# Attention and two dense blocks: row maxima of the third and fourth query tile, one instruction per head

## Chip, cores and metric

The kernel runs on one core of one Trainium2 chip. The metric is the device time of one execution in microseconds (us). A core has five engines that work side by side, each through its own queue and in the order of that queue: TensorE (PE, matrix products), VectorE (DVE), ScalarE (ACT), GpSimd (POOL) and SyncE (SP, which here only issues transfers). They wait for each other with semaphores.

## What is computed

The reference is causal attention with a memory term, and two dense blocks behind it. The part that the change touches is the softmax of the attention:

```python
B, H, S, D = q.shape                       # 4, 8, 576, 64
scores = scale * np.matmul(q, k.transpose(0, 1, 3, 2))
scores = np.where(causal, -1000000000.0, scores)
scores = scores - scores.max(-1, keepdims=True)
a = np.exp(scores)
a /= a.sum(-1, keepdims=True) + 1e-09
local = np.matmul(a, v)
...
x = _moe_ref(x=x, **moe_kwargs)            # ((x @ w1) * (x @ w2)) @ w3 @ w_out
return _moe2_ref(x=x, **moe2_kwargs)       # h = x @ w_in; (h - tanh(h)) @ w_out
```

The attention's result is mixed with the memory term by a gate of each head before the dense blocks.

## The kernel before

The work runs in three stages. In the first, the attention, the 32 pairs of batch and head are taken two heads at a time: 16 pairs P, each with 576 queries cut into five query tiles. A unit n is one pair and one query tile u, so there are 80 units. For u from 0 to 3 a tile holds 128 queries and sees K = 128 (u + 1) keys; u = 4 holds the last 64 queries of both heads, one head on each half of the partitions. The second stage is the first dense block (with the rest of the memory term), the third is the second dense block.

For a unit the steps are these, with the names that the loop over `ORDER` uses:
- S: `scores` (PE) writes both heads' scores into a PSUM tile `sc` of [128, 2, 512], one bank for each head, and adds the causal mask by a product with the identity. There are two such tiles, so the scores of unit n + 2 need the tile of unit n. Then `rmax` (line 343, DVE) takes the negated maximum of each row into the tile `st`; one instruction reads both heads and writes two columns.
- E: `exps` (line 352, ACT) has one instruction for each head: the exponential of the scores with the maximum as bias, written to `p`, and the row sum into a further column of `st` (for u = 4 one instruction for both heads). In the trace each is followed by a short read of the accumulator.
- N: `norm` adds 1e-9 to the sums and takes the reciprocal (lines 361 and 362, DVE), and POOL scales `p` (line 369).
- T: `trans` (lines 401 to 412), one unit later: PE transposes `p`, and ACT or DVE copies the result out of PSUM (lines 380, 382).
- A: `av`, two units later: the products with v.
- L loads the q/k tile of a later pair and scales the next pair's q (line 196, ACT).
- G: background work from a generator, some two steps for each unit: the decoder of the 64-bit weights, whose steps alternate between ACT (line 74), DVE (lines 75, 77, 81, 84) and POOL (lines 96, 99), the product of two weight matrices (tiles `fo`, `s`, `wf`, lines 257 to 263), and the memory term of the first group of tokens (tiles `mw`, `mst`, lines 491 to 529).

The generator's instructions carry an edge that puts them behind the unit's own marked instruction on DVE and on ACT (`mark["V"]`, `mark["A"]`, used by `issue_after`). Beyond such edges, the order in each engine's queue is not that of the program: the context is opened with `schedule_with_timeline_sim=True`, which orders the instructions by a modelled timeline when the program is built. A change in the instructions can so change the order of others.

The lines that the change touches and those that read what it writes:

```python
mark["V"][n] = DV.tensor_reduce(out=st[:, 0:2] if u < 4 else st[:, 0:1], in_=seen(n),
                                axis=AX.X if u < 4 else AX.XY, op=ALU.max, negate=True).ins
...
for x in [slice(0, 1), slice(1, 2)] if u < 4 else [slice(0, 2)]:
    mark["A"][n] = AC.activation(out=p[:, x], in_=sc[:, x], func=AF.Exp, bias=st[:, x.start:x.start + 1],
                                 accum_out=st[:, 2 + x.start:3 + x.start]).ins
```

Of the kernel before, what the change touches and what calls it, by code (L numbers as in the profile page):

```python
# [18 lines left out]
ALU = mybir.AluOpType  # L19
AX = mybir.AxisListType  # L20
# [12 lines left out]
def block_kernel(ctx, tc, qk, qt, vt, mp, zp_d, beta, w1, w2, w3t, wo, wi, wo2, ident_d, mask_d, out):  # L33
    nc = tc.nc
    PE, DV, AC, PO, SP = nc.tensor, nc.vector, nc.scalar, nc.gpsimd, nc.sync
# [143 lines left out]
    V = [ap1.tile([128, 5, 2, 64], F32, name=f"v{i}") for i in range(2)]  # L179
# [87 lines left out]
    if True:  # L267
# [48 lines left out]
        mark = {"V": {}, "A": {}}  # L316
# [19 lines left out]
        def seen(n):  # L336
            P, u = units[n]
            return sc_t[n][:, :, 0:128 * (u + 1) if u < 4 else 288]

        def rmax(n):  # L340
            P, u = units[n]
            st = st_t[n] = ap4.tile([128, 8], F32, tag="st", name="st")
            mark["V"][n] = DV.tensor_reduce(out=st[:, 0:2] if u < 4 else st[:, 0:1], in_=seen(n),  # L343
                                            axis=AX.X if u < 4 else AX.XY, op=ALU.max, negate=True).ins

        def exps(n):
            P, u = units[n]
# [229 lines left out]
        def do(x, n):  # L577
# [3 lines left out]
            if x == "S":  # L581
                scores(n)
                rmax(n)
            elif x == "E":
                exps(n)
            elif x == "N":
                norm(n)
            elif x == "T":
                trans(n)
            elif x == "A" and u in (1, 4):  # L590
                av(P, u // 4)
                if u == 4 and P + 2 < 16:
                    load_v(P + 2)
            elif x == "L":
                if u == 0 and 1 <= P <= 16 - RB:
                    load_qk(P + RB - 1)
                if u == 2 and P < 15:
                    scale_q(P + 1)
            elif x == "G":
                bgc[0] += BG if n < MB else BG2  # L600
                with ExitStack() as s:
                    for e, k in TH:
                        if n - k >= 0:
                            s.enter_context(tc.issue_after(mark[e][n - k]))
                    while bgc[0] >= 1:
                        if next(bg, None) != 1:
                            bgc[0] -= 1
# [363 lines left out]
```

## Time and profile before

| what | value |
|---|---|
| median of 3 runs | 1025.48 us (1024.51 to 1026.22) |
| the profiled execution's own time | 1025.37 us |
| its span, first to last instruction | 1023.6 us |
| busy share of the span | PE 95%, DVE 74%, ACT 58%, POOL 36% |
| reductions of line 343 | 80 instructions, 63.8 us of DVE in all |
| exponentials of line 352 | 144 instructions, 78.3 us of ACT in all |
| ACT idle ahead of exponentials, ended by line 343 | 30.5 us, 32 times |
| granted TensorE clock | 0.995 of full speed over the span |

The profile is of one execution. Busy times are unions of an engine's instructions, so two that overlap count once. A wait is put down to the instruction that ended last before it. The chain of waits is followed back from the last instruction of the program: at each step to what released it, or to the instruction before it on its engine. `st<-sc` means that tile `st` is written from tile `sc`; shapes are partitions x elements. The attention stage takes about the first 256 us.

### The profile page before, as it was taken

Reading aid. Unit: us, or ns where it says so; the run is one execution under the profiler, and the core shown is the slowest. Engines: PE = TensorE matmul, PEld = TensorE weight load, DVE = VectorE, ACT = ScalarE, POOL = GpSimd, SP = SyncE. Lnnn points to the kernel's source line nnn. Section 1 sums busy time; section 2 is a strip of 40 time slices with the busy share of each in tenths; the row PEclk is TensorE's granted clock in tenths of the full one; section 3 lists DMA queues with packets and bytes.
Section 4 is the critical chain, followed back from the end, with each engine's and each line's share of the span. In section 5 each row is a group of like instructions: output and inputs, shape, how many; then the busy total and the mean of one; then the engine's idle time right before and its main releaser. Section 6 shows DMA issues by size and latency. Waiting matters only on the chain.

```text
span 1023.6 us, 15593 instructions
## 1 busy us (share of the span) xinstructions
PE 976.3 (95%) x5512; PEld 823.4 (80%) x5512; DVE 758.0 (74%) x1361; ACT 593.1 (58%) x1356; POOL 364.4 (36%) x396
## 2 busy tenths in 40 slices
PE   5999999989987989999999999999999999999998
PEld 2565565544876778999999989999999999989996
DVE  5868888787689996575212798878787787788875
ACT  5767766677323434233222458777676677767765
POOL 3646756486465212200000773222222222221221
PEclk9999999999999999999999999999999999999999
DMA  6434543343144652133000100000000000000000
GB/s 227 133 109 144 167 150 101 114 133 93 45 152 128 186 180 63 52 124 103 1 1 1 42 21 1 1 1 31 1 32 1 1 32 1 32 1 1 32 1 31
DMA packets 44237, 68.27 MB, mean 67 GB/s; under 512 B 4864, under 2 KB 30208, under 8 KB 44160
## 3 DMA queue, kind: packets, MB, share of 16 engines
q1 hardware_dynamic: 44160, 67.29, 20.8%
q8 instruction: 43, 0.70, 0.3%
q14 instruction: 34, 0.28, 0.1%
HBM read 62.56 MB, written 4.72 MB: 66 GB/s over the span
## 4 chain that ended last, share of the span: by engine, by line
PE 69%; DVE 18%; ACT 4%; issue 4%; DMA 3%; POOL 1%; SPq 0%; DVEq 0%; ACTq 0%; POOLq 0%
PE o L143 22%; PE h L143 20%; PE ab L143 13%; PE x L143 6%; DVE T L81 3%; PE sc L143 3%; PE fo L143 3%; DVE st L343 2%; DVE T L75 2%; ACT p L352 2%; DVE T L77 2%; PE t L401 2%; DMA r<-in_qk 1%; DVE T L84 1%; DMA mw<-in_qt 1%
## 5 line engine op out<-in xcount | busy, mean ns | idle before, releaser
L858 POOL TENSOR_TENSOR gl<-s,gh 128x384 fp32r<-128x384 f32 x96 | 99.8, 1039 | 295.3 <-ACT gh L852 286.3
L143 PE MATMUL ab<-xh,wa 128*128 128x384 f32 x384 | 108.6, 343 | 8.2 <-DVE xs L529 4.1
L369 POOL TENSOR_SCALAR p<-p,st 128x128 f32<-128x128 f32 (+2 forms) x144 | 94.2, 666 | 54.7 <-DVE st L362 21.7
L143 PE MATMUL x<-abh,wf 128*128 128x384 f32 x384 | 106.9, 342 | 2.7 <-ACT abh L656 2.1
L143 PE MATMUL ab<-xh,wb 128*128 128x384 f32 x384 | 106.2, 337 | 0.5 <-POOL wb L96 0.5
L352 ACT ACTIVATE p<-sc,st 128x128 f32<-128x128 f32 (+2 forms) x144 | 78.3, 549 | 45.1 <-DVE st L343 30.5
L834 DVE SCALAR_TENSOR_TENSOR s<-s,u 128x384 f32<-128x384 f32 x96 | 84.1, 876 | 22.8 <-ACT s L824 21.7
L143 PE MATMUL sc<-r 64*64 64x288 f32 (+4 forms) x384 | 76.1, 479 | 16.8 <-ACT p L352 11.0
L830 ACT ACTIVATE u<-u,pc 128x384 f32<-128x384 f32 x96 | 59.4, 619 | 46.5 <-DVE s L834 46.5
L74 ACT ACTIVATE T<-raw 128x512 f32<-128x512 f32 x72 | 48.2, 674 | 64.0 <-DMA raw<-in_wo 9.4
L653 DVE TENSOR_TENSOR a<-ab,a 128x384 f32<-128x384 f32 x48 | 26.5, 551 | 76.6 <-PE ab L143 76.6
L143 PEld LDWEIGHTS ab<-xh,wa 128*128 128x128 f32 x384 | 70.9, 190 | 12.4 <-DVE xs L529 5.3
L343 DVE TENSOR_REDUCE st<-sc 128x2 f32<-128x256 f32 (+4 forms) x80 | 63.8, 799 | 18.5 <-PE sc L143 17.3
L840 DVE TENSOR_TENSOR t<-h,t 128x384 f32<-128x384 f32 x96 | 53.3, 555 | 32.1 <-ACT t L823 31.7
L822 ACT ACTIVATE u<-h 128x384 f32<-128x384 f32 x96 | 47.0, 490 | 48.5 <-PE h L143 48.5
L143 PEld LDWEIGHTS x<-abh,wf 128*128 128x128 f32 x384 | 70.3, 189 | 4.5 <-ACT abh L656 3.2
L143 PEld LDWEIGHTS ab<-xh,wb 128*128 128x128 f32 x384 | 70.7, 189 | 1.2 <-POOL wb L96 1.2
L143 PE MATMUL x<-abl,wf 128*128 128x384 f32 x192 | 66.2, 345 | 3.9 <-DVE abl L657 3.9
L839 DVE SCALAR_TENSOR_TENSOR s<-s,s 128x384 f32<-128x384 f32 x96 | 62.9, 655 | 8.7 <-DVE s L834 0.5
L143 PE MATMUL ab<-xl,wa 128*128 128x384 f32 x192 | 65.5, 342 | 1.5 <-DVE xl L633 1.5
L846 DVE COPY_PREDICATED s<-u,t 128x384 f32<-128x384 uint32 x96 | 58.4, 609 | 9.0 <-ACT t L823 0.5
L143 PE MATMUL ab<-xl,wb 128*128 128x384 f32 x192 | 64.5, 336 | 0.0
(214 smaller groups left out, 2587.7 us busy)
## 6 DMA issues: line engine op xcount, KB each, us to landing
raw<-in_wo SPq DMA_DIRECT2D x24, 512.0 KB, 3.5
r<-in_qk SPq DMA_DIRECT2D x15, 576.0 KB, 3.9
raw<-in_w3t SPq DMA_DIRECT2D x16, 512.0 KB, 3.7
raw<-in_w SPq DMA_DIRECT2D x16, 512.0 KB, 3.8
raw<-in_wi SPq DMA_DIRECT2D x16, 512.0 KB, 3.7
v<-in_vt SPq DMA_DIRECT2D x16, 320.0 KB, 3.9
mw<-in_qt SPq DMA_DIRECT2D x18, 256.0 KB, 3.2
out<-ob SPq DMA_DIRECT2D x18, 256.0 KB, 2.3
```

Of the source, the lines that this page charges most:

```text
L74: AC.activation(out=tf, in_=hw.bitcast(F32), func=AF.Abs)
L143: return PE.matmul(o, lhsT, rhs, start=start, stop=stop).ins
L343: mark["V"][n] = DV.tensor_reduce(out=st[:, 0:2] if u < 4 else st[:, 0:1], in_=seen(n), axis=AX.X if u < 4 else AX.XY, op=ALU.max, negate= ...
L352: mark["A"][n] = AC.activation(out=p[:, x], in_=sc[:, x], func=AF.Exp, bias=st[:, x.start:x.start + 1], accum_out=st[:, 2 + x.start:3 + x. ...
L369: (DV if NV[u] == "V" else PO).tensor_scalar(out=pr, in0=pr, scalar1=sc, scalar2=1.0, op0=ALU.mult, op1=ALU.mult)
L822: AC.activation(out=u, in_=o, func=AF.Square)
L830: AC.activation(out=u, in_=u, func=AF.Relu, bias=pc[:, 2:3])
L834: DV.scalar_tensor_tensor(out=s1, in0=s1, scalar=k2[0], in1=u, op0=ALU.add, op1=ALU.mult)
L839: DV.scalar_tensor_tensor(out=s1, in0=s2, scalar=k2[1], in1=s1, op0=ALU.add, op1=ALU.mult)
L840: DV.tensor_tensor(out=t, in0=o, in1=t, op=ALU.subtract)
L846: DV.copy_predicated(out=s1, mask=u[:].bitcast(U32), data=t)
L858: PO.tensor_tensor(out=l, in0=s1, in1=h[:].bitcast(F32), op=ALU.subtract)
```

## The change

For u = 2 and u = 3 the maxima are taken by two instructions, the first over head 0's scores into the first column of `st`, the second over head 1's into the second column. The unit's mark on DVE is then the second of them. The other units keep one instruction (for u = 4, `seen(n)[:, x]` with the slice 0 to 2 is what `seen(n)` was).

```diff
         def rmax(n):
             P, u = units[n]
             st = st_t[n] = ap4.tile([128, 8], F32, tag="st", name="st")
-            mark["V"][n] = DV.tensor_reduce(out=st[:, 0:2] if u < 4 else st[:, 0:1], in_=seen(n),
-                                            axis=AX.X if u < 4 else AX.XY, op=ALU.max, negate=True).ins
+            for x in [slice(0, 1), slice(1, 2)] if u in (2, 3) else [slice(0, 2)]:
+                mark["V"][n] = DV.tensor_reduce(out=st[:, x] if u < 4 else st[:, 0:1], in_=seen(n)[:, x],
+                                                axis=AX.X if u < 4 else AX.XY, op=ALU.max, negate=True).ins
```

## Rows read from the trace of the kernel before

**Rows 1.** All instructions of line 343: durations in ns, first and last start in us.
```profile
L343 DVE TENSOR_REDUCE st<-sc x80: 398/742/1225, 5.2 to 251.3; 128x2 f32<-128x256 f32 x16, 128x2 f32<-128x512 f32 x16, 128x2 f32<-128x768 f32 x16, 128x2 f32<-128x1024 f32 x16
```

**Rows 2.** Busy us of each engine by stretch, with its instructions (x); then clock, DMA.
```profile
89.00:117.00 28.00, 27.52 (x189) 16.32 (x188) 24.70 (x52) 21.37 (x62) 20.24 (x28) 1.00 0.46 149
...
139.00:180.00 41.00, 39.22 (x246) 24.44 (x244) 36.29 (x70) 25.56 (x71) 24.46 (x30) 1.00 0.38 117
180.00:193.00 13.00, 12.83 (x82) 8.67 (x84) 7.58 (x22) 8.69 (x25) 5.64 (x9) 1.00 0.29 91
193.00:238.00 45.00, 38.82 (x287) 21.47 (x286) 41.60 (x93) 33.32 (x97) 32.42 (x41) 1.00 0.47 148
```

**Rows 3.** Chain of waits, 89 to 238 us: start us, us on the chain, what.
```profile
92.78 0.84 DVE st L343
...
93.70 0.12 ACT p L352
...
235.88 0.86 DVE st L343
...
236.83 1.24 ACT p L352 x4
```

**Rows 4.** Groups of line 343 by shape: count | busy us, mean ns | idle before.
```profile
L343 DVE TENSOR_REDUCE st<-sc 128x2 f32<-128x1024 f32 x16 | 19.4, 1216 | 1.2 <-PE sc L143 0.9 <-PE t L412 0.3
...
L343 DVE TENSOR_REDUCE st<-sc 128x2 f32<-128x768 f32 x16 | 15.1, 944 | 1.7 <-POOL zs L99 0.9 <-PE sc L143 0.8
...
L343 DVE TENSOR_REDUCE st<-sc 128x2 f32<-128x512 f32 x16 | 10.9, 679 | 2.5 <-PE sc L143 2.5
...
L343 DVE TENSOR_REDUCE st<-sc 128x2 f32<-128x256 f32 x16 | 6.6, 415 | 6.8 <-PE sc L143 6.8
```

**Rows 5.** Timeline of DVE from 177.97 us: start us, us, instruction.
```profile
177.97 1.21 DVE L343 TENSOR_REDUCE st<-sc 128x2 f32<-128x1024 f32 x1
179.10 0.41 DVE L77 TENSOR_SCALAR T<-T 128x512 uint32<-128x512 uint32 x1
...
180.04 0.74 DVE L343 TENSOR_REDUCE st<-sc 128x1 f32<-128x576 f32 x1
...
181.33 0.14 DVE L361 TENSOR_SCALAR st<-st 128x2 f32<-128x2 f32 x1
```

**Rows 6.** Timeline of ACT, exponentials of u = 2; idle us before in brackets.
```profile
107.61 0.58 ACT L352 ACTIVATE p<-sc,st 128x384 f32<-128x384 f32 x1 [0.76 <-DVE st L343]
...
108.19 0.57 ACT L352 ACTIVATE p<-sc,st 128x384 f32<-128x384 f32 x1
...
173.65 0.58 ACT L352 ACTIVATE p<-sc,st 128x384 f32<-128x384 f32 x1 [0.23 <-DVE st L343]
...
208.95 0.58 ACT L352 ACTIVATE p<-sc,st 128x384 f32<-128x384 f32 x1 [0.54 <-DVE st L343]
```

**Rows 7.** Timeline of DVE, instructions behind eight idle gaps, 89 to 238 us.
```profile
95.53 1.02 DVE L75 TENSOR_SCALAR T<-T 128x512 f32<-128x512 f32 x1 [0.19 <-ACT T L74]
...
100.82 0.46 DVE L75 TENSOR_SCALAR T<-T 128x512 f32<-128x512 f32 x1 [0.22 <-ACT T L74]
...
108.88 0.43 DVE L361 TENSOR_SCALAR st<-st 128x2 f32<-128x2 f32 x1 [1.36 <-ACT p L352]
...
144.69 0.63 DVE L361 TENSOR_SCALAR st<-st 128x2 f32<-128x2 f32 x1 [0.71 <-ACT p L352]
...
161.19 0.17 DVE L361 TENSOR_SCALAR st<-st 128x2 f32<-128x2 f32 x1 [0.71 <-ACT p L352]
...
174.91 0.25 DVE L361 TENSOR_SCALAR st<-st 128x2 f32<-128x2 f32 x1 [0.42 <-ACT p L352]
...
210.22 0.20 DVE L361 TENSOR_SCALAR st<-st 128x2 f32<-128x2 f32 x1 [1.36 <-ACT p L352]
...
224.66 1.20 DVE L75 TENSOR_SCALAR T<-T 128x512 f32<-128x512 f32 x2 [0.37 <-ACT T L74]
```

**Rows 8.** Chain of waits at the start: the first pair's remaining q/k columns.
```profile
5.24 9.62 DMA r<-in_qk
```

## The prediction

> **What bounds the kernel now.** I read first the busy time of each engine by stretch, because the change sits in the first quarter of the span, the attention stage: its reductions start between 5.2 and 251.3 us [rows 1]. No engine rules that stage alone. TensorE (PE) is busy nearly throughout, 27.52 of 28 us and 39.22 of 41 us in two stretches, but a busy PE counts latencies that overlap. VectorE (DVE) is busy 24.70 of 28 us (88%), 36.29 of 41 (89%) and 41.60 of 45 (92%) in the stretches from 89, 139 and 193 us, and only 7.58 of 13 from 180 us, where PE leads [rows 2]. The chain of waits, read next, agrees: in these three stretches it runs over DVE and ScalarE (ACT). Between 89 and 238 us it steps ten times from a reduction of a third or fourth tile (u = 2, 3) to the exponentials of the same unit, first at 92.78 us and last at 235.88 us [rows 3]. So two things count: how long DVE is occupied, and how soon after a reduction starts ACT can begin. I call those the DVE stretches; they hold 17 of the 32 reductions that the change touches.
>
> About 0.2% (2 us) is what a measurement of this kernel can tell from no change.
>
> **What is added.** 32 reductions (u = 2 and 3 in 16 pairs) become 64. The four shapes lie on a line: 415 ns for 256 elements, 679 for 512, 944 for 768, 1216 for 1024 [rows 4]. That is (1216 - 415) / 768 = 1.04 ns an element and some 148 ns that don't depend on the size. A half of u = 2 has 384 elements: (415 + 679) / 2 = 547 ns; a half of u = 3 has 512: 679 ns. The two halves take 2 x 547 - 944 = 150 ns and 2 x 679 - 1216 = 142 ns more than one instruction, by their recorded durations.
>
> Not all of it is occupancy. The reduction at 177.97 us takes 1.21 us and its successor begins at 179.10, so 177.97 + 1.21 - 179.10 = 0.08 us overlap [rows 5]. A second half costs 150 - 80 = 70 or 142 - 80 = 62 ns of DVE, mean 66. All 32: 2.1 us; without any overlap 32 x 146 ns = 4.7 us. I take the 66 ns, as the overlap is read from a reduction followed by an independent instruction, which is what the second half is. Queued behind it are the unit's normalisation, the copies and the decoder's steps on DVE; whoever waits for these (GpSimd's splits of the weights, PE's next product) waits 0.07 us longer where DVE has no gap.
>
> Here a page speaks against the change. The trace charges 66 ns of occupancy, as just worked out. The Trainium skill (VectorE: DVE Perf Modes, the section on the TRN2 errata) holds that many small tiles pay a fixed charge each, advises at least 512 elements, and gives 120 cycles at 0.96 GHz for PSUM sources; the halves of u = 2 fall short of that. As an estimate from that page, 32 x 125 ns = 4.0 us would be added, nearly the no-overlap end.
>
> On ACT no instruction is added; the second exponential now has a wait of its own. It meets it: the two exponentials of u = 2 start 0.58 us apart, at 107.61 and 108.19, the first of them 0.09 us behind its reduction, which DVE ended at 108.88 - 1.36 = 107.52 [rows 6, 7]. After the change the second is due 547 + 90 + 580 = 1217 ns from the start of the reduction, and its maximum is there at 2 x 547 - 80 = 1014. For u = 3 it is due at 679 + 90 + 580 = 1349 or later, its exponential being longer, against 2 x 679 - 80 = 1278. I cost this wait at nothing; if the first exponential's time did not cover it, each saving below would shrink by what the second maximum is late. No DMA is added or moved on any queue.
>
> **What is moved.** The first exponential can start when the first half is done, 944 - 547 = 0.40 us earlier for u = 2 and 1216 - 679 = 0.54 us for u = 3. It is worth that only if ACT stood idle, and to the end only if DVE then stands idle for the result. I went through the idle gaps of DVE in the DVE stretches and kept those which a unit of u = 2 or 3 feeds [rows 7]; ACT's own idle time before those exponentials caps each (0.23 us at 173.65, and 0.54 at 208.95 as the smallest of the others [rows 6]).
> - 95.53 and 100.82 us: a decoder step waits for ACT, which was held by the exponentials before; the whole gaps, 0.19 and 0.22, go.
> - 108.88 us, gap 1.36, u = 2: 0.40. 144.69, gap 0.71, u = 3: 0.54.
> - 161.19, gap 0.71: ACT is carried forward by the u = 2 exponentials before it, 0.40. 174.91, gap 0.42: 0.23 by ACT's cap.
> - 210.22, gap 1.36, u = 2: 0.40. 224.66, a decoder step again: the whole 0.37.
>
> Sum: 0.19 + 0.22 + 0.40 + 0.54 + 0.40 + 0.23 + 0.40 + 0.37 = 2.75 us.
>
> Five of these gaps (108.88, 144.69, 161.19, 174.91, 210.22) stay open and swallow their own 66 ns; the other 12 splits of the DVE stretches pay: 12 x 0.066 = 0.79 us. Net gain 2.75 - 0.79 = 1.96 us. The 15 splits outside lie where PE leads or the start waits for loads; DVE has room there (7.58 of 13 us), so I cost them at nothing. If that cover were gone they would add 15 x 0.066 = 1.0 us. What is late next, once the gaps are shorter, is DVE's own decoding work and PE, which in the first stretch has only 28 - 27.52 = 0.48 us to give against 0.81 us that I take there.
>
> After 256 us nothing is changed; what the attention stage gains passes on whole unless its tail is rearranged.
>
> **The sum.** The profiled execution took 1025.37 us (its span 1023.6 and 1.8 around it), 0.11 below the median of 1025.48. 1025.37 - 1.96 = **1023.4 us**. The bounds: all ten steps of the chain saved in full and none of the 0.79 paid is 7 x 0.40 + 3 x 0.54 = 4.4 us, or 1021.0; nothing saved and everything paid without overlap is 1030.1.
>
> **Rivals.**
> - **DVE takes it back (slower).** In the DVE stretches DVE has ready work behind most reductions: after the one at 177.97 us three further instructions follow without a gap [rows 5]. If the gaps that I shorten are refilled by work that then runs later, the added occupancy decides: 32 x 0.066 = 2.1 us to 4.7 us, 1027.5 to 1030.1. It decides from the point where the gaps removed fall below 0.8 us, the cost of the 12 uncovered splits. Against it: eight gaps are there, and five stay open after what is taken. Chance 0.15.
> - **PE is the bound, no change.** PE's 27.52 of 28 and 39.22 of 41 us speak for it; then the savings of the stretches from 89 and 139 us are lost and at most 0.40 + 0.37 us of the third stay, 1024.6 to 1025.4. Against it speaks the chain, which in these stretches rarely touches PE. Chance 0.15.
> - **The planner reorders.** The order on each engine comes from a modelled timeline, not from the program: the reduction of the fifth unit at 180.04 us runs ahead of the fourth unit's normalisation at 181.33, which the program writes first [rows 5]. With other modelled costs many instructions can change places. The size of one such move is a gap of [rows 7], up to 1.36 us, and three in one direction make 4 us: 1019.4 or 1027.4 after the forecast. Chance 0.20, with more of it on the fast side (0.14 to 0.06), since a planner that sees earlier exponentials can use them.
> - **It doesn't do what it says.** If waits were kept for a whole tile, the first exponential would wait for both halves, and 32 x 0.066 to 0.146 us would only be added (1027.5 to 1030.1). Against it: the first reduction starts at 5.2 us [rows 1], while the rest of the same q/k tile is still landing, from 5.24 for 9.62 us [rows 8]; waits go by region. I leave it in the first rival's chance.
>
> **How the numbers follow.** The forecast's case has 0.50; it straddles the 2 us bound (1021.0 to 1025), and I give 0.31 of it to faster and 0.19 to same. Faster: 0.31 + 0.14 = 0.45. Same: 0.19 + 0.15 = 0.34. Slower: 0.15 + 0.06 = 0.21. The range from 1018.5 to 1028.0 takes in the planner's fast end with 0.9 to spare for the other gaps, and the lower end of the slower rival; its far part is left out. Within it the forecast's own range is 1021.0 to 1025.0.
>
> **What would show it.** In the profile after: 112 reductions on that line, with 32 of 384 elements near 547 ns and 32 of 512 near 679 ns in one column each; second halves starting 0.08 us before the first ones' recorded end; first exponentials some 0.1 us behind the first half; the gaps of [rows 7] shorter by the amounts listed; DVE's busy total up by about 2 us; the last reduction starting some 2 us before 251.3. I would be wrong if the first exponential started behind the second half, if the last reduction came no sooner, or if the queues were in another order, so that the gaps cannot be matched one to one.

## The result, and the profile after

The changed kernel takes 1032.58 us (median of 4 runs, 1030.74 to 1033.79); the kernel before took 1025.07 us beside it (4 runs). The ratio is 1.0070, with a 95% interval of 1.0052 to 1.0088. So the change is slower by 7.5 us, where 1023.4 us was forecast and the range ended at 1028.0 us. In a later session, against ten runs of before, the same kernel gave 1.0052 (below). A part of the loss lies outside the span from first to last instruction: the runs of the changed kernel take 2.1 to 2.2 us beside their span, where those of before take 1.7 to 1.9; the forecast kept 1.8. Why is not known.

The added instructions are what was reckoned with. The groups of the reduction's line by shape, which is now line 344 (all lines behind it are one higher too), answer to [rows 4]; busy us and mean ns of one stand behind the first bar:

```profile
L344 DVE TENSOR_REDUCE st<-sc 128x1 f32<-128x512 f32 x32 | 20.5, 680 | 2.5 <-PE sc L143 2.5
L344 DVE TENSOR_REDUCE st<-sc 128x1 f32<-128x384 f32 x32 | 16.4, 546 | 2.8 <-PE sc L143 1.9 <-POOL zs L99 0.9
```

There are 32 and 32 halves of 680 and 546 ns (679 and 547 were worked out). But all instructions of the line begin their last one 6.9 us later than in [rows 1], at 258.2 instead of 251.3 us. The second line, from the same view, counts who waited for the reductions:

```profile
L344 DVE TENSOR_REDUCE st<-sc x112: 396/674/759, 5.5 to 258.2; 128x1 f32<-128x384 f32 x32, 128x1 f32<-128x512 f32 x32, 128x2 f32<-128x256 f32 x16, 128x2 f32<-128x512 f32 x16
...
  ACT p L353: 27.2, 33
```

The busy time by stretch answers to [rows 2] (PE, PEld, DVE, ACT and POOL, each with its instructions; then clock, DMA):

```profile
89.00:117.00 28.00, 28.00 (x186) 16.38 (x182) 25.31 (x57) 20.64 (x59) 19.28 (x27) 1.00 0.43 138
139.00:180.00 41.00, 40.42 (x246) 25.64 (x246) 32.75 (x68) 25.01 (x66) 22.34 (x30) 1.00 0.35 101
180.00:193.00 13.00, 11.70 (x85) 7.21 (x82) 9.43 (x23) 7.94 (x23) 7.00 (x8) 1.00 0.43 140
193.00:238.00 45.00, 38.25 (x264) 21.55 (x262) 39.69 (x94) 30.78 (x88) 28.59 (x38) 0.96 0.37 119
```

In the stretch from 139 us DVE is now busy for 32.75 of 41 us, where it was 36.29: it has more to do and does less, so it waits. (The stretches are cut by time, and the changed kernel is some 2 us behind by then, so they don't hold quite the same work.) The next view is the timeline of one unit with u = 2 (pair 6), the one that [rows 6] and [rows 7] show at 107.61 and 108.88 us. Columns: start us, us, engine, instruction, and the idle time before it with its releaser; x2 is two instructions shown as one.

```profile
107.24 1.02 DVE L344 TENSOR_REDUCE st<-sc 128x1 f32<-128x384 f32 x2
...
108.35 0.59 ACT L353 ACTIVATE p<-sc,st 128x384 f32<-128x384 f32 x1 [0.75 <-DVE st L344]
...
108.93 0.57 ACT L353 ACTIVATE p<-sc,st 128x384 f32<-128x384 f32 x1
...
109.62 0.94 DVE L362 TENSOR_SCALAR st<-st 128x2 f32<-128x2 f32 x1 [1.36 <-ACT p L353]
```

The two halves end at 107.24 + 1.02 = 108.26 us, and the first exponential begins 0.09 us after that, not after the first half. DVE's gap behind it is 1.36 us as before. It is so in all 32 split units: the first exponential begins at least 0.09 us after the end of the **second** half (0.09 also in the median), and at least 0.56 us after the end of the first. The early start that the forecast counted is not there.

That explains why nothing was gained, not a loss of 7.5 us. For it, the order of the queues was compared. If the reductions of line 343 or 344 are left out, both traces hold the same records (1281 on DVE, 1356 on ACT, 5512 on PE, 396 on POOL), but at least 58 on DVE, 52 on ACT, 171 on PE and 15 on POOL don't stand in the same relative order (so many are left over by the longest sequence that both have in common). So two theories went to the chip: the added instructions cost the time, or the new order of the queues does.

### The profile page after: what moved, and what is told of

Read it like the earlier page. It is cut to its first block, busy times and chain, and to the rows that moved or that the text cites. A ratio compares the mean times of both kernels' runs of the same rounds, so it can differ in the third digit from the quotient of the medians.

```text
span 1031.6 us, 15619 instructions
## 1 busy us (share of the span) xinstructions
PE 982.3 (95%) x5512; PEld 825.3 (80%) x5512; DVE 764.9 (74%) x1393; ACT 592.8 (57%) x1356; POOL 356.9 (35%) x396
## 4 chain that ended last, share of the span: by engine, by line
PE 75%; DVE 15%; issue 3%; DMA 3%; ACT 2%; POOL 1%; SPq 0%; DVEq 0%; ACTq 0%; POOLq 0%
PE o L143 23%; PE h L143 19%; PE ab L143 13%; PE x L143 6%; PE sc L143 5%; PE fo L143 4%; PE t L402 3%; DVE T L81 3%; DMA mw<-in_qt 2%; DVE T L75 2%; DVE st L344 2%; DVE T L77 2%; DVE T L84 1%; ACT p L353 1%; PE mo L143 1%
## 5 line engine op out<-in xcount | busy, mean ns | idle before, releaser
L370 POOL TENSOR_SCALAR p<-p,st 128x128 f32<-128x128 f32 (+2 forms) x144 | 91.7, 650 | 59.3 <-DVE st L363 27.6
L143 PE MATMUL sc<-r 64*64 64x288 f32 (+4 forms) x384 | 79.3, 481 | 17.8 <-ACT p L353 12.1
L344 DVE TENSOR_REDUCE st<-sc 128x1 f32<-128x384 f32 (+4 forms) x112 | 66.2, 613 | 21.6 <-PE sc L143 20.5
L81 DVE SCALAR_TENSOR_TENSOR T<-raw,T 128x512 uint16<-128x512 uint32 x72 | 66.4, 925 | 0.9
```

Of the source, the lines that this page charges most:

```text
L81: DV.scalar_tensor_tensor(out=l16, in0=lw, scalar=2.0 ** -29, in1=l16, op0=ALU.mult, op1=ALU.add)
L143: return PE.matmul(o, lhsT, rhs, start=start, stop=stop).ins
L344: mark["V"][n] = DV.tensor_reduce(out=st[:, x] if u < 4 else st[:, 0:1], in_=seen(n)[:, x], axis=AX.X if u < 4 else AX.XY, op=ALU.max, neg ...
L370: (DV if NV[u] == "V" else PO).tensor_scalar(out=pr, in0=pr, scalar1=sc, scalar2=1.0, op0=ALU.mult, op1=ALU.mult)
```

## Experiments

Kernels "in the order of before" are built twice: first the kernel before alone, whose order on each engine is noted, then the kernel in question, with an edge without a semaphore from each instruction to its predecessor in that order, and each second half directly behind its first. In their traces no record of PE, ACT, DVE or POOL is out of the old order. The pinning adds no instruction and no wait that the trace shows: the kernel with a single split in the old order (below) has as many records as the kernel before, 15593, and no engine waits more often. Each run states its ratio to runs of the kernel before on the same chip.

### Order or instructions

**The split in the old order, and the old reductions in the new order.** In both, the body of the loop can take a tile whole or by heads:

```diff
+for x in [slice(0, 1), slice(1, 2)] if SPLIT(P, u) else [slice(0, 2)]:
+    ... DV.tensor_reduce(out=st[:, x] ..., in_=seen(n)[:, x], ...)
...
+order = trace(scratch, arrays, lambda P, u: ORDER_OF)     # first build
+trace(nc, arrays, lambda P, u: SPLIT_OF, order)           # second, pinned
```

In the first kernel ORDER_OF is False and SPLIT_OF is u in (2, 3); in the second it is the other way round.

> The 64 halves of the change, with every engine's queue held in the order of the kernel before (order edges between neighbours of a queue; the second half stands right behind the first). Theory 'order' (the loss comes from the planner's new order, the halves themselves are worth the 2 us of the prediction): 1021 to 1025 us, and the last reduction starts 0 to 4 us before 251.3. Theory 'instruction' (32 more instructions on DVE and later second maxima cost the time themselves): 1030 to 1034 us, as in the changed kernel.

> The 32 whole reductions of the kernel before, with every queue held in the order that the changed kernel has (a whole reduction stands where the two halves stood). Theory 'order': 1031 to 1037 us, as slow as the changed kernel or some 2 us slower. Theory 'instruction': 1024 to 1027 us, as the kernel before.

Measured: the split in the old order 1027.94 us, ratio 1.0016 (1.0005 to 1.0027). The whole reductions in the new order, with not one instruction more than the kernel before: 1031.58 us, ratio 1.0052 (1.0040 to 1.0064). The order alone makes most of the loss. Where it arises is seen by the start of the first exponential of some units, in us: before, and how much later (+) or sooner it is in other kernels (the last two are experiments further below).

| unit (pair, u) | before | changed | whole, new order | whole_signal | head_signal |
|---|---|---|---|---|---|
| 6, 3 | 112.39 | +1.32 | +0.69 | +0.05 | -1.80 |
| 7, 0 | 116.73 | +2.99 | +2.35 | +0.06 | -1.50 |
| 7, 3 | 126.78 | +1.26 | +0.64 | +0.14 | -1.52 |
| 10, 3 | 179.28 | +3.99 | +2.99 | +0.14 | -2.94 |
| 13, 0 | 217.54 | +2.47 | +1.49 | +1.88 | -0.32 |
| 13, 3 | 225.73 | +5.67 | +4.92 | +1.97 | -0.50 |
| 15, 3 | 251.06 | +6.89 | +5.20 | +2.92 | -1.50 |

The changed kernel and the old reductions in its order are late at the same units, in jumps, and not by a little at every split. Two cautions go with the table. A unit that comes late is not yet a loss: the jump at unit 7, 0 is made up by unit 7, 3, and only what the last row shows has stayed. And stretches of low clock (last section) fall on some rows: one at 217.52 us in the whole reductions' execution, one at 232.66 us in the changed kernel's, and one each at 180.16 and 179.07 us in those of the last two columns, where both jump between 10, 3 and 13, 0. The changed kernel's 3.2 us between 13, 0 and 13, 3 have full clock. How a new order makes a unit late is seen at the jump to unit 7, 0; which of the moves leave a loss behind was not traced. The timelines there, of the kernel before:

```profile
114.75 0.49 PE L143 MATMUL sc<-r 64*128 64x128 f32 x4
...
115.30 0.61 PE L401 MATMUL t<-ident,p 128*128 128x128 f32 x4
...
115.83 0.41 DVE L343 TENSOR_REDUCE st<-sc 128x2 f32<-128x256 f32 x1
...
116.16 0.58 DVE L77 TENSOR_SCALAR T<-T 128x512 uint32<-128x512 uint32 x1
...
116.73 0.39 ACT L352 ACTIVATE p<-sc,st 128x128 f32<-128x128 f32 x1
```

and of the whole reductions in the new order:

```profile
115.61 1.09 PE L401 MATMUL t<-ident,p 128*128 128x128 f32 x8
...
116.63 0.49 PE L143 MATMUL sc<-r 64*128 64x128 f32 x4
...
117.35 1.30 DVE L77 TENSOR_SCALAR T<-T 128x512 uint32<-128x512 uint32 x1
...
118.57 0.41 DVE L344 TENSOR_REDUCE st<-sc 128x2 f32<-128x256 f32 x1
...
119.08 0.37 ACT L352 ACTIVATE p<-sc,st 128x128 f32<-128x128 f32 x1 [1.15 <-DVE st L344]
```

Before, PE puts pair 7's first scores ahead of four transposes, and DVE takes the reduction ahead of the decoder's step of line 77. In the new order the scores stand behind eight transposes and come at 116.63 instead of 114.75 us, and the reduction stands behind that step and starts at 118.57 us. ACT is then idle for 1.15 us. Nothing here is slower; it is queued differently.

**Only u = 2, and only u = 3**, with the order left to the planner:

```diff
-for x in [slice(0, 1), slice(1, 2)] if u in (2, 3) else [slice(0, 2)]:
+for x in [slice(0, 1), slice(1, 2)] if u == 2 else [slice(0, 2)]:    # the other kernel: u == 3
```

> Only the third tile (u = 2) is taken head by head, the planner is free. Theory 'order': anywhere from 1019 to 1035 us, and the differences of this run and of the next to the kernel before need not add up to the 7.5 us of the whole change. Theory 'instruction': about half of it, 1028 to 1030 us.

> Only the fourth tile (u = 3) is taken head by head, the planner is free. Theory 'order': anywhere from 1019 to 1035 us, not the remainder of 7.5 us after the run with u = 2 alone. Theory 'instruction': about half, 1028 to 1030 us, so that both differences add up to 7 to 8 us.

Measured: 1031.29 us, 1.0051 (1.0037 to 1.0066), and 1029.87 us, 1.0032 (1.0020 to 1.0043). The losses don't add: 5.0 and 3.6 us for half of the splits each, where both together cost 4.7 to 7.5. Each has an order of its own (at least 30 and 34 records of DVE out of the old order).

**One split alone**, that of pair 11's third tile, planner free and in the old order:

```diff
-for x in [slice(0, 1), slice(1, 2)] if u in (2, 3) else [slice(0, 2)]:
+for x in [slice(0, 1), slice(1, 2)] if (P, u) == (11, 2) else [slice(0, 2)]:
```

> Of the 32 units only one (pair 11, u = 2, near 194 us) is taken head by head; one more instruction on DVE, some 0.07 us. Its queues are those of the kernel before up to there, and some 200 instructions of PE's queue stand elsewhere behind it. Theory 'order': 1.5 to 5 us slower than the kernel before, all of it behind 190 us. Theory 'instruction': the same time within 0.3 us.

> The changed kernel once more, beside the others on the same chip: 6 to 9 us slower than the kernel before by either theory; it gives the size that the parts must add up to here.

> One split alone, that of pair 11's third tile, as in the run that left the order free (1.0046), but every queue keeps the order of the kernel before, with the second half directly behind the first. Theory (the order is what costs): within 0.3 us of the kernel before, ratio 0.9990 to 1.0010, the one added instruction costing 0.07 us or nothing. Rival (the extra instruction itself, or a signal that it adds, hits a critical place): over 2 us slower, as with the free order.

Measured: free 1030.99 us, 1.0046 (1.0031 to 1.0061), beside the changed kernel on the same chip at 1030.51 us, 1.0052 (1.0032 to 1.0072). In the old order 1027.18 us, 1.0013 (1.0003 to 1.0023). One added instruction of 0.55 us moves at least 27 records of DVE, 22 of ACT and 51 of PE, and costs about as much as 32 of them. In the old order most of that is gone. What is left, 1.0 us, is a little over what I had allowed, but in the profiled execution it is not the split's: the first exponentials are 0.67 us ahead of before's at unit 10, 4 (181 us) and 0.89 us late at unit 11, 0 (188 us), behind a stretch of low clock from 179.52 us (last section). The split unit, 11, 2, adds 0.06 to that.

**Only u = 1**, planner free, a control: the order hardly changes (8 records of DVE, 8 of ACT, 16 of PE, none of POOL).

```diff
-for x in [slice(0, 1), slice(1, 2)] if u in (2, 3) else [slice(0, 2)]:
+for x in [slice(0, 1), slice(1, 2)] if u == 1 else [slice(0, 2)]:
```

> The second tiles (u = 1) of all pairs are taken head by head instead, 16 added instructions as when only u = 2 or only u = 3 is split, with the order left free; but here the order stays nearly that of the kernel before (30 instructions out of their old relative order on all engines, where splitting u = 2 has 318). Theory (order): within 1.5 us of the kernel before, ratio 0.999 to 1.0015. Rival (16 instructions and their later exponentials cost 3 to 5 us by themselves, as u = 2 alone and u = 3 alone did): ratio 1.003 to 1.005.

Measured: 1029.21 us, 1.0031 (1.0017 to 1.0044), outside what the theory of the order allowed. A small reordering is no guarantee of a small cost, or these splits cost more than those of u = 2 and 3 in the old order; one profile doesn't tell which. That profile is of the slowest of the 12 runs (1032.44 us). In it the delay is 1.3 us by unit 10, 3; at a stretch of low clock at 27.91 us it goes from -0.5 (unit 1, 2) to +0.7 (unit 1, 4), and the later steps again meet such stretches, at 181.51 and 229.29 us. This stays open.

### The wait for the second half

**The second half behind the first exponential**, with its own small tile for the maximum, in the old order and with the order free:

```diff
 for x in [slice(0, 1), slice(1, 2)] ...:
+    half(n, x) if x.start and SPLIT(P, u) else None     # second maximum, into sh
     AC.activation(out=p[:, x], in_=sc[:, x], ..., bias=(sh_t[n] if x.start else st)[...])
```

> Halves and order as in split_old_order, but the second half writes a tile of its own and is traced between the two exponentials, so that in the built program the first exponential waits for the first half alone and the second half for nothing of ACT. Theory 'late release' (the halves with the old order brought nothing because the first exponential still waited for the second half; with its own wait the sum of the prediction holds): some 2 us under the kernel before, 1022 to 1025 beside 1026, and 3 us or more under split_old_order. Rival 'absorbed' (an earlier exponential only lengthens the next wait): as split_old_order within 1 us, 0 to 2 us above the kernel before.

> The same halves with the early release, the planner free. Theory 'order is a draw' (a new order costs what its own collisions cost, whatever the edit saves): between 3 us faster and 7 us slower than the kernel before, most likely slower, and not the time of early_old_order. Rival 'the planner uses the early exponential': 2 to 6 us faster than the kernel before.

Measured: 1050.91 us, 1.0244 (1.0223 to 1.0265), and 1032.99 us, 1.0071 (1.0047 to 1.0094). My expectation was wrong about this kernel: the second half does wait for ACT. The timeline of the first split unit in the old order:

```profile
14.58 0.54 DVE L344 TENSOR_REDUCE st<-sc 128x1 f32<-128x384 f32 x1
...
15.71 0.57 ACT L352 ACTIVATE p<-sc,st 128x384 f32<-128x384 f32 x1
...
16.41 0.56 DVE L344 TENSOR_REDUCE sh<-sc 128x1 f32<-128x384 f32 x1 [1.29 <-ACT p L352]
...
17.00 0.58 ACT L352 ACTIVATE p<-sc,sh 128x384 f32<-128x384 f32 x1 [0.62 <-DVE sh L344]
```

Half, exponential, half, exponential: each waits for the one before, though the maxima lie in two tiles and the scores of the two heads in two banks. The only thing that the second half and the first exponential share is the tile `sc`, which both only read. So the wait comes with that tile: in this program two engines take turns at one PSUM tile, whichever bank of it they read. That also accounts for the changed kernel, where the second half stands first. There `st` is shared as well; the next pair, which keeps both maxima in one `st`, rules it out.

**Two tiles of one bank.** Here `sc` is two tiles, every u is taken by heads, u = 4 with two reductions, a minimum and two exponentials. The pair has the same instructions in the same order (that of before); the second of them has an edge that makes the first exponential of u = 2 and 3 wait for the second half.

```diff
-sc = sc_t[n] = pss.tile([128, 2, 512], F32, tag="sc", name="sc")
+sc = sc_t[n] = [pss.tile([128, 512], F32, tag=f"sc{h}", name=f"sc{h}") for h in range(2)]
...
+tc.add_manual_dep(first_exp, second_half.name, Sync)   # u in (0, 1); in the partner all u < 4
```

> The scores of a unit lie in two tiles of one bank each instead of one tile of two banks, every unit's maxima are taken head by head, and every engine's queue keeps the order of the kernel before. Of u = 2 and 3 the first exponential waits only for its own head's maximum; of u = 0 and 1 both exponentials wait for both maxima. The fifth tile (u = 4) takes two reductions, a minimum and two exponentials where it had one of each. The run is half of a pair with the next one, which differs in one wait alone. Both theories: first exponentials of u = 2 and 3 begin about 0.1 us behind the end of the first half and before the end of the second. Theory A (the change would have paid as forecast, had the first half signalled): this run is 2.75 us under its partner (the sum over eight DVE gaps), ratio of the two 0.997. Rival B (the early start is absorbed, since ACT then waits at its next unit or DVE's gaps are refilled): within 0.5 us of its partner. Against the kernel before, with 48 more splits and 32 more instructions at u = 4 than the change has: by A 1024 to 1027, by B 1027 to 1031.

> The same instructions in the same order as the run before it, with one more wait: the first exponential of u = 2 and 3 also waits for the second head's maximum, as in the changed kernel. First exponentials begin about 0.1 us behind the end of the second half. Theory A: 2.75 us over its partner. Rival B: within 0.5 us of its partner. Against the kernel before: 1027 to 1031 by both.

Measured: early 1028.44 us, 1.0026 (1.0014 to 1.0039); late 1033.30 us, 1.0074 (1.0059 to 1.0088). In the early kernel's trace the first exponential of u = 2 and 3 begins 0.10 us (median) behind the end of its own half, in the late one's 0.09 us behind the second. The early start is worth 4.9 us here, more than the 2.75 us of the gap list. Against the kernel before, the extra work at u = 0, 1 and 4 can hide that; the next pair is free of it.

**The change as it was meant.** The scores stay in one tile; the first exponential is declared independent of the second half. That is sound, as the two read different banks and write different columns of `st`.

```diff
     mark["A"][n] = AC.activation(out=p[:, x], in_=sc[:, x], func=AF.Exp, ...).ins
+    tc.declare_no_dep(mark["A"][n], second_half.name, ...)   # first exponential of u = 2, 3
```

> The change on the scores tile as it is, every queue in the order of the kernel before, and the first exponential of u = 2 and 3 declared to be independent of the second half, so that it waits for its own head's maximum alone. One wait apart from its partner whole_signal. Theory (the prediction's mechanism was right and only the signal was missing): first exponentials about 0.1 us behind the first half; 3 to 5 us under the partner, as the pair with two tiles showed 1028.4 against 1033.3 us; so 0.998 to 0.996 of the kernel before, 1022 to 1024 us. Rival (the gain of the two-tile pair came from its extra work at the other tiles, which the early start only hid): within 1 us of the partner and not under the kernel before.

> The partner of head_signal: the same instructions in the same order, the first exponential of u = 2 and 3 waiting for both halves. It is the kernel of split_old_order, run again on this chip. By both theories 1.000 to 1.003 of the kernel before, as it was (1.0016).

Measured: 1024.86 us, 0.9978 (0.9967 to 0.9990), faster than the kernel before; its partner 1028.88 us, 1.0012 (1.0003 to 1.0021), as when it ran first. One wait apart, they differ by 4.0 us (their means by 3.8, give or take 1.0). The same unit as above, in whole_signal:

```profile
106.48 1.02 DVE L344 TENSOR_REDUCE st<-sc 128x1 f32<-128x384 f32 x2
...
107.60 0.58 ACT L352 ACTIVATE p<-sc,st 128x384 f32<-128x384 f32 x1 [1.01 <-DVE st L344]
...
108.17 0.57 ACT L352 ACTIVATE p<-sc,st 128x384 f32<-128x384 f32 x1
...
108.86 0.36 DVE L361 TENSOR_SCALAR st<-st 128x2 f32<-128x2 f32 x1 [1.36 <-ACT p L352]
```

and in head_signal:

```profile
105.60 1.02 DVE L344 TENSOR_REDUCE st<-sc 128x1 f32<-128x384 f32 x2
...
106.25 0.58 ACT L352 ACTIVATE p<-sc,st 128x384 f32<-128x384 f32 x1 [0.56 <-POOL p L369]
...
106.82 0.57 ACT L352 ACTIVATE p<-sc,st 128x384 f32<-128x384 f32 x1
...
107.51 0.38 DVE L361 TENSOR_SCALAR st<-st 128x2 f32<-128x2 f32 x1 [0.90 <-ACT p L352]
```

From the start of the first half to the first exponential it is 106.25 - 105.60 = 0.65 us instead of 1.12, and DVE's gap is 0.90 instead of 1.36 us. (The view names POOL as the releaser of the exponential, because the shown end of the two halves, 106.62, lies behind its start; it begins 0.10 us behind the end of the first half.) The second exponential follows the first without a gap. From 106.25 to 106.62 us ACT reads one bank of the tile and DVE the other. The Trainium skill (PSUM — Partial Sum Buffer, the summary of rules for kernel authors) advises, for reading PSUM while a matmul runs, to target a different bank and to guard by bank. Here both engines are readers, and this trace shows them in two banks of one tile at once; with a guard by bank the wait for the whole tile would not have been needed.

**The same, with the order left to the planner**, and **with u = 0 and 1 too**, in the old order:

```diff
 # head_signal_free: the changed kernel and the declaration, no order given
 # head_signal_all, second build:
-trace(nc, arrays, lambda P, u: u in (2, 3), order)
+trace(nc, arrays, lambda P, u: u < 4, order)
```

> The changed kernel with the same declaration and with the order left to the planner, which now reckons with the earlier exponentials; its queues differ from the order of before about as much as those of the changed kernel do. Theory (order and signal are two separate terms): the order costs some 5 us and the signal gives 3 to 5 back, so 0.999 to 1.002 of the kernel before, 3 to 7 us over head_signal. Rival (the planner's orders were bad only because the exponentials were late): as fast as head_signal, 0.996 to 0.998.

> As head_signal, with u = 0 and 1 taken head by head too (32 more halves), order of before. A half of u = 0 or 1 comes 0.13 or 0.27 us sooner than the whole by the slope of the four shapes, and each split adds some 0.07 us to DVE. If the early start counts wherever DVE isn't full: up to 1.5 us under head_signal. If the added 32 x 0.066 = 2.1 us of DVE count more: 1 to 2 us over it. I expect it 1 us over.

Measured: free 1030.62 us, 1.0029 (1.0018 to 1.0041), 5.8 us over head_signal. The planner's order costs about as much with early exponentials as with late ones (5.3 us above). With all of u < 4: 1022.84 us, **0.9954** (0.9941 to 0.9966), the fastest of all, 4.6 us under the kernel before. I had expected it 1 us over head_signal; it is 2.0 us under, of which 0.4 lie outside the span (1.8 us beside it, where head_signal has 2.2). The first exponentials of the two profiles differ by 0.2 to 0.6 us from unit 0, 2 to unit 10, 3; the rest lies where the two executions met low clock at different places, and isn't settled.

## Why the prediction was wrong

**The step that failed first** is "The first exponential can start when the first half is done". It was drawn from "waits go by region": the first reduction runs while the rest of the same q/k tile lands [rows 8]. That row was misread. The transfer at 5.24 us is of the next pair's whole tile: what it releases is line 196 on 576 columns, at 14.89 us. The first pair's remaining 448 columns were issued at 2.56 us and were scaled at 6.38 us:

```profile
2.56 0.57 SPq L189 DMA_DIRECT2D r<-in_qk  x1
...
5.24 0.46 SPq L189 DMA_DIRECT2D r<-in_qk  x1
...
6.38 0.58 ACT L196 ACTIVATE r<-r 128x448 f32<-128x448 f32 x1
...
14.89 0.68 ACT L196 ACTIVATE r<-r 128x576 f32<-128x576 f32 x1 [0.76 <-DMA r<-in_qk]
```

For that tile the reading still holds, as these columns landed at 6.36 us and the first reduction starts at 5.19. But the tile lies in SBUF and is written by transfers. The scores lie in PSUM, and there the first exponential waits for both halves, 32 times out of 32. The rival "It doesn't do what it says" named exactly this and was dismissed on that one row. Its own time, 1027.5 to 1030.1 us, would have been nearly right for the instructions alone (ratios 1.0016 and 1.0012 in the old order).

**The step that failed by more** is the planner's rival. I had the mechanism and one row for it, but gave it 0.20, mostly on the fast side, and at most three gaps, 4 us. The order alone costs 5.3 us (whole reductions, new order) or 5.8 us (head_signal_free over head_signal). One jump in the table above is 3.2 us (changed kernel, between units 13, 0 and 13, 3). All seven kernels for which the planner made an order anew were slower than the kernel before, by 0.3 to 0.7%. I have no rule that explains why, and whether the order of before is simply a good draw was not tested; with one row of [rows 5] as evidence, the sign should not have been taken as known. The two terms, 1.5 us for the splits and 5.3 for the order, make 6.8 us, within what was measured (4.7 to 7.5 us in two sessions). The prediction held these two rivals for alternatives, each with a time of its own; both came at once.

**Sound in its other steps, once the wait was gone and the order kept.** The forecast was 1023.4 of 1025.48 us, or 0.9980; head_signal measured 0.9978. That they agree so closely is partly luck: the gain from the early start was larger than forecast (3.31 us of gaps, 4.0 us by the medians, for 2.75), and so was the cost of the splits (1.5 us for 0.79).
- *Occupancy.* From the start of the first half to the end of the second it takes 1.008 us for u = 2 and 1.280 for u = 3 in the mean (whole_signal), where the whole took 0.944 and 1.216 [rows 4]: 0.064 us more in both, against 0.066 reckoned. By the Trainium skill (VectorE: DVE Perf Modes, the section on the TRN2 errata) the estimate was 4.0 us for all splits, from its 120 cycles for PSUM sources (the advice of 512 elements stands there for SBUF sources); that would be a ratio of 1.0039, outside the intervals of both runs of the split in the old order, which give 1.5 us. Of these 1.5 us, 0.35 lie outside the span (2.1 to 2.2 us beside it instead of 1.8), a term that the prediction did not have.
- *The second exponential's wait* costs nothing, as reckoned: it starts when the first one ends (0.01 us before its recorded end in the median; only at unit 5, 3 does it start 0.26 us later, and so it did before).
- *The eight gaps* of [rows 7] are in head_signal 0, 0, 0.90, 0.12, 0.11, 0, 0.90 and 0 us. That is 0.19 + 0.22 + 0.46 + 0.59 + 0.60 + 0.42 + 0.46 + 0.37 = 3.31 us less, where 2.75 was forecast. The cap by ACT's idle time at 174.91 us (0.23) was too low: the whole 0.42 us went. In whole_signal none of the eight changed by over 0.02 us.
- *The splits outside* cost nothing: in whole_signal the first exponentials are 0.33 us ahead of before's at unit 2, 0 and 0.36 at unit 5, 0, with six splits between. head_signal is 1.14 us ahead at unit 5, 0, but hardly by the early start: 0.99 us of that it has at unit 0, 1, ahead of the first split unit, since a load of weights let line 74 begin at 9.89 us in that execution and at 10.89 in that of before. With the lead at unit 0, 1 taken off, the one wait is worth 2.11 us by unit 10, 0 (head_signal from -0.99 to -2.58, whole_signal from -0.54 to -0.02), and the five gaps up to there give 2.06. So up to there, with full clock in both executions, the gap list accounts for the gain. Behind that it is less clean: head_signal_all loses 0.9 us of its lead between units 9, 4 and 10, 4, also at full clock, and why was not traced. Nor is it settled why the medians differ by 4.0 us. A part may be the clock: head_signal's runs have a mean granted clock of 0.9920, whole_signal's 0.9905, which by the last section's 0.35 us for each 0.001 is 0.5 us, as an estimate.
- *"PE is the bound"* fell: in head_signal PE is busy for 27.86 of the 28 us from 89 us, and the time is gained all the same. So near to full, a busy PE still was no bound.

## What to carry to other kernels

A finer instruction helps only if its end is signalled: look in the trace for the first waiting instruction behind the end of the *first* part, and remember that, as here, reads of one PSUM tile by two engines may be put in turn even where their banks differ. Where a planner orders the queues, compare the orders before costs, and pin the old order to see what an edit does by itself; one added instruction of 0.55 us cost 0.46% here with the order that followed from it, and 0.13% with the order kept. A gap list of the bottleneck engine predicted the gain well (2.75 against 3.31 us), once the mechanism was real.

## Not expected of the hardware

In the attention stage of these profiles TensorE's granted clock falls to half (1.2 GHz) for 3.41 or 6.83 us at a time, and at other places in other executions. In the profiled execution of the kernel before it did so at no place between 20 and 256 us. In that of whole_signal it did at 180.16 and 227.95 us. The busy time by stretch around the first (the clock is the number behind POOL's count):

```profile
172.00:180.00 8.00, 6.14 (x36) 3.62 (x34) 6.71 (x16) 4.91 (x13) 4.42 (x6) 1.00 0.33 109
180.00:184.00 4.00, 3.71 (x16) 1.80 (x18) 2.56 (x8) 2.69 (x9) 1.48 (x3) 0.57 0.30 98
```

and in the kernel before, with the same order of instructions:

```profile
172.00:180.00 8.00, 6.21 (x36) 3.70 (x34) 6.70 (x14) 5.06 (x15) 4.42 (x6) 1.00 0.33 101
180.00:184.00 4.00, 3.83 (x24) 2.42 (x25) 2.44 (x8) 2.44 (x8) 1.60 (x3) 1.00 0.38 119
```

PE was busy for 6.14 and 6.21 of the 8 us ahead (for 4.00 of the first 4 us in both, and for 2.14 and 2.21 of the last 4), and yet the clock was 0.57 in one and 1.00 in the other; 24 products became 16, and the delay of the first exponentials went from +0.26 us (unit 10, 4) to +1.68 (unit 11, 0). Over the 29 runs of the kernel before that stood beside the two-tile pair, the time falls as the mean granted clock rises (0.982 to 0.997, correlation -0.77, 0.35 us for each 0.001). So one profile can lay 1.4 us at the door of a place where the kernel did nothing differently, and differences under 2 us were read from the medians here.
